# Attention and an MLP on one core: v loaded first, zeros for TensorE, new bounds for w_out, a new order

## The chip, the cores and the metric

The kernel runs on one NeuronCore of one Trainium2 chip. The metric is the device time of one execution in microseconds, as the median of a few runs. The engines work side by side and wait for each other by semaphores: TensorE (PE in the profile; its weight loads are PEld), VectorE (DVE), ScalarE (ACT), GpSimd (POOL) and SyncE (SP), which here issues all DMAs.

## The reference

```python
# q, k, v: 4 batches, 12 heads, 448 rows, 64 columns, float32
scores = scale * np.matmul(q, k.transpose(0, 1, 3, 2))
scores = np.where(mask, -1000000000.0, scores)        # causal
scores = scores - np.max(scores, axis=-1, keepdims=True)
attn = np.exp(scores)
attn = attn / (np.sum(attn, axis=-1, keepdims=True) + 1e-09)
attn_out = np.matmul(attn, v)
x = attn_out.transpose(0, 2, 1, 3).reshape(1792, 768)
h = x @ w_in                                          # w_in: 768 x 2048, float64 in memory
g = h - np.tanh(h)
return g @ w_out                                      # w_out: 2048 x 768, float64 in memory
```

## The kernel before

**Numbers.** Every large product is made of float16 matmuls. An operand is scaled by a power of two and split into a high and a low float16 part (`split`: one pass for the high part, `scaled`, and one for the low one), and three products replace one (high x high, high x low, low x high). The scale needs a bound of the operand's size first. For x, v, q and k it is a reduction or a pass (`bound`) and a small matmul that carries the maximum across partitions (`over_partitions`), followed by `bound_scale`. For w_in and w_out it is `magnitudes`: groups of matmuls of the operand with itself into the bank `b_scales`, whose maximum VectorE reads; `root_scale` makes the scale of it. The weights lie in memory as 64-bit floats. `decode` turns a loaded piece (the tile `slot` or `e`) into 32-bit floats: one shift pass (VectorE, ScalarE or GpSimd), then twice one ScalarE pass (into the banks that the trace calls `b_s`) and one VectorE pass.

**Stages.** (1) `first_rows` for batches 0 and 1, the chunk `c`: attention of the first 128 rows of each batch, in float32, in units of four heads (three units per batch, six per chunk). A unit is four score matmuls in float32, of which the trace shows two records each, eight in all (`b_s<-g`), four softmax parts on VectorE and ScalarE, `inverse` of the sums, the multiplication by it (`p0`), four transposes into a bank, the copy out of it (`p0t`), four value matmuls (eight records) into a bank, and the split of the result into x (`x0`). One bank, `b_x`, takes the transposes and the values in turn. (2) `w_in_chunk`, eight times: load, decode, magnitudes, scale, split of 256 columns of w_in. (3) `first_rows` for batches 2 and 3, the chunk `c2`. (4) `mlp_g_first`: x times w_in for both chunks, tanh, the split of g (`g0`, `g2`). (5) `w_out_half`, twice: sixteen pieces of w_out in all. (6) `mlp2` of both chunks: g times w_out. (7) For each batch, attention of the other 320 rows (`prep`, `weights_unit`, `weights_last`, `values`), then x times w_in (`mlp_g`) and g times w_out. The inverses of the sums (`inverse`, 75 of them, 12 in the first rows) stand between the softmax and the split of the weights.

**Order.** The instructions are not issued as written. The class `Work` collects them, and `schedule` plays them on a model of the engines (prices in `cost`, latencies in `LAT` and others) and takes, on each engine, the operation of the lowest rank among those that are ready by then. The ranks come from `RANK`. Where an operation can run on several engines (`either`), the letters of `CFG` say which one takes each occurrence: V is VectorE, A ScalarE, G GpSimd. What the model yields is fixed in the program as the order of each engine's queue; the chip works each queue off in order. All loads go through SyncE's queue in that fixed order. Every instruction is issued at one line, 288 of the file, so the trace's rows are told apart by tile, not by line.

## Time and profile before

| | us |
|---|---|
| median of 3 runs (581.05 to 581.48) | 581.06 |
| the profiled execution | 579.8 |
| its span, first to last instruction | 578.1 |

| engine | busy us | share of the span | instructions |
|---|---|---|---|
| PE | 557.8 | 96% | 5296 |
| PEld | 382.2 | 66% | 5296 |
| DVE | 426.5 | 74% | 1207 |
| POOL | 341.9 | 59% | 428 |
| ACT | 286.5 | 50% | 751 |

The shares are means over the whole span, over stages with different limits. A matmul's own duration includes its way through the pipeline, so groups of them are best read from the start of one group to the start of the next. In the rows, `b_m` are the banks of the MLP's products, `b_s` those of scores (and of the decode), `b_x` that of transposes and values, `small` the small columns for scales and sums.

### The profile page before, as it was taken

Reading aid. Unit: us, or ns where it says so; the run is one execution under the profiler, and the core shown is the slowest. Engines: PE = TensorE matmul, PEld = TensorE weight load, DVE = VectorE, ACT = ScalarE, POOL = GpSimd, SP = SyncE. Lnnn points to the kernel's source line nnn. Section 1 sums busy time; section 2 is a strip of 40 time slices with the busy share of each in tenths; the row PEclk is TensorE's granted clock in tenths of the full one; section 3 lists DMA queues with packets and bytes.
Section 4 is the critical chain, followed back from the end, with each engine's and each line's share of the span. In section 5 each row is a group of like instructions: output and inputs, shape, how many; then the busy total and the mean of one; then the engine's idle time right before and its main releaser. Section 6 shows DMA issues by size and latency. Waiting matters only on the chain.

```text
span 578.1 us, 13879 instructions
## 1 busy us (share of the span) xinstructions
PE 557.8 (96%) x5296; PEld 382.2 (66%) x5296; DVE 426.5 (74%) x1207; ACT 286.5 (50%) x751; POOL 341.9 (59%) x428
## 2 busy tenths in 40 slices
PE   6789999999999999999999999999999999999997
PEld 4567888866565666766666766566776566776664
DVE  5899999989999999699969996958599382332000
ACT  6899785744766845562555341606445150332000
POOL 3548965633563878975887888487956930542000
PEclk9999999999999999999999999999999999999999
DMA  8998379835486774365544435946123354000100
GB/s 305 343 298 310 112 213 258 239 110 178 102 161 136 183 163 78 93 174 124 119 118 92 92 66 109 211 100 125 42 69 62 69 80 101 2 1 1 28 28 27
DMA packets 109283, 74.04 MB, mean 128 GB/s; under 512 B 89760, under 2 KB 93344, under 8 KB 108704
## 3 DMA queue, kind: packets, MB, share of 16 engines
q1 hardware_dynamic: 109216, 73.15, 49.7%
q8 instruction: 41, 0.67, 0.5%
q14 instruction: 26, 0.21, 0.1%
HBM read 45.61 MB, written 5.51 MB: 88 GB/s over the span
## 4 chain that ended last, share of the span: by engine, by line
PE 68%; DVE 14%; DMA 7%; POOL 4%; issue 3%; ACT 2%; SPq 1%; DVEq 0%; POOLq 0%; ACTq 0%
PE b_m L288 57%; PE b_x L288 5%; PE b_s L288 5%; DVE pn L288 3%; DVE slot L288 2%; DVE small L288 2%; DVE prob L288 1%; PE b_scales L288 1%; DMA e<-in_v_dram 1%; DMA slot<-in_first_dram 1%; DMA g<-in_first_dram 1%; DVE g L288 1%; DVE first L288 1%; POOL first L288 1%; DMA pt<-pn 1%
## 5 line engine op out<-in xcount | busy, mean ns | idle before, releaser
L288 PE MATMUL b_m<-x,w_in 128*128 128x320 f16 (+1 forms) x1728 | 229.6, 290 | 1.6 <-DVE small L288 1.0
L288 PEld LDWEIGHTS <-w_in 128*128 128x128 f16 x1728 | 165.9, 98 | 56.3 <-issue 7.8
L288 PE MATMUL b_m<-slot,g 128*128 128x384 f16 x1152 | 191.7, 326 | 0.6 <-DVE t L288 0.5
L288 PEld LDWEIGHTS <-g 128*128 128x128 f16 x1152 | 111.1, 98 | 76.5 <-issue 5.1
L288 ACT ACTIVATE prob<-prob,small 128x256 f32<-128x256 f32 (+2 forms) x102 | 58.5, 574 | 62.2 <-DVE small L288 62.2
L288 ACT ACTIVATE t<-b_m,small 128x320 f32<-128x320 f32 (+1 forms) x70 | 37.6, 537 | 63.1 <-PE b_m L288 56.0
L288 DVE SCALAR_TENSOR_TENSOR t<-b_m,small,t 128x320 f32<-128x320 f32 (+1 forms) x70 | 39.4, 564 | 30.9 <-ACT t L288 30.7
L288 DVE CUSTOM_DVE_ANT_0 prob<-b_s,mask,small 128x384 f32<-128x384 f32 (+1 forms) x87 | 44.9, 549 | 8.6 <-PE b_s L288 7.5
L288 DVE TENSOR_SCALAR small<-small 128x1 f32<-128x1 f32 (+5 forms) x190 | 43.4, 242 | 6.1 <-ACT o L288 5.2
L288 ACT ACTIVATE o<-b_m,small 128x384 f32<-128x384 f32 x21 | 12.0, 572 | 61.3 <-PE b_m L288 61.3
L288 POOL TENSOR_SCALAR prob<-prob,small 128x384 f32<-128x384 f32 (+2 forms) x46 | 29.2, 634 | 18.9 <-ACT pn L288 6.6
L288 POOL TENSOR_SCALAR t<-t,small 128x320 f32<-128x320 f32 (+1 forms) x41 | 25.6, 625 | 23.9 <-ACT g L288 12.3
L288 POOL TENSOR_TENSOR g<-t,g 128x320 f16<-128x320 f32 (+1 forms) x40 | 34.1, 852 | 3.3
L288 PEld LDWEIGHTS <-v 128*64 128x64 f16 x1296 | 31.1, 111 | 7.1 <-issue 7.1
L288 DVE SCALAR_TENSOR_TENSOR pn<-prob,small,pn 128x256 f16<-128x256 f32 (+2 forms) x45 | 33.7, 767 | 1.5 <-ACT pn L288 0.8
L288 DVE SCALAR_TENSOR_TENSOR slot<-b_s,e 128x384 int32<-128x384 int32 x64 | 33.7, 548 | 0.9 <-POOL e L288 0.4
L288 PE MATMUL b_m<-slot,first 128*128 128x384 f16 x192 | 33.9, 326 | 0.0
L288 PE MATMUL b_s<-k,q 64*128 64x256 f16 (+2 forms) x342 | 30.6, 317 | 0.1
L288 POOL TENSOR_SCALAR g<-t,small 128x320 f16<-128x320 f32 (+1 forms) x21 | 14.5, 690 | 27.3 <-DVE t L288 25.9
L288 PEld LDWEIGHTS <-first 128*128 128x128 f16 (+2 forms) x282 | 21.7, 98 | 13.4 <-issue 2.2
L288 POOL TENSOR_TENSOR pn<-prob,pn 128x384 f16<-128x384 f32 (+2 forms) x30 | 28.0, 934 | 2.5
L288 POOL TENSOR_SCALAR e<-slot 128x768 int32<-128x768 uint16 x19 | 20.0, 1050 | 14.3 <-DMA slot<-in_moe_w_in_dram 6.6
(165 smaller groups left out, 878.8 us busy)
## 6 DMA issues: line engine op xcount, KB each, us to landing
slot<-in_moe_w_in_dram SPq DMA_DIRECT2D x16, 768.0 KB, 6.3
slot<-in_qk_dram SPq DMA_DIRECT2D x18, 384.0 KB, 3.4
slot<-in_moe_w_out_dram SPq DMA_DIRECT2D x8, 768.0 KB, 4.5
e<-in_moe_w_out_dram SPq DMA_DIRECT2D x8, 768.0 KB, 4.5
e<-in_v_dram SPq DMA_DIRECT2D x3, 1536.0 KB, 6.9
out_dram<-o SPq DMA_DIRECT2D x24, 192.0 KB, 1.9
first<-in_qk_dram SPq DMA_DIRECT2D x6, 384.0 KB, 3.7
g<-in_first_dram SPq DMA_DIRECT2D x6, 256.0 KB, 4.9
```

What stands on the lines that cost most here:

```text
L288: getattr(self.eng[o["eng"]], method)(*args, **kw)
```

## The change

- `first_rows` issues both loads of v before those of q and k, with a rank of their own (`c0_v`, `c0b_v`). For the chunk `c` the transposes and values use three banks in turn (`b_x` and the two `b_m`); for `c2` still one.
- A memset on GpSimd and 32 matmuls of zeros, 128x256 in bfloat16, into a `b_m` bank, with the rank 1002.08, which is behind all others.
- The bounds of w_out: instead of `magnitudes` (six matmuls per piece) and a reduction of 128 columns, one pass over the decoded piece (128x768) by `bound`: the sum of the absolute values on ScalarE for 14 pieces, their maximum on VectorE for 2. Its scale comes from `bound_scale`.
- The magnitudes of w_in are added up in one block of 128 columns instead of two, so that the reduction behind them reads 128 columns instead of 256.
- Small operations (`h`, 48 of them, and `inverse`) can go to GpSimd: 11 and 27 do.
- The model's prices and latencies, the ranks, how far the model looks ahead, and the letters are new, and so is the order of all queues.

The letters, counted as VectorE / ScalarE / GpSimd:

| operation | count | before | after |
|---|---|---|---|
| `p0` | 12 | 1 / 0 / 11 | 0 / 0 / 12 |
| `p0t` | 12 | 0 / 12 / 0 | 12 / 0 / 0 |
| `x0` | 12 | 1 / 11 / 0 | 3 / 9 / 0 |
| `g0`, `g0_lo` | 8, 8 | 2 / 0 / 6, 2 / 0 / 6 | 8 / 0 / 0, 0 / 0 / 8 |
| `g2`, `g2_lo` | 8, 8 | 0 / 5 / 3, 6 / 0 / 2 | 0 / 1 / 7, 3 / 0 / 5 |
| `shift_in` | 16 | 0 / 0 / 16 | 1 / 2 / 13 |
| `shift_out` | 16 | 2 / 6 / 8 | 0 / 5 / 11 |
| `w_out`, `w_out_lo` | 16, 16 | 1 / 10 / 5, 13 / 0 / 3 | 1 / 15 / 0, 14 / 0 / 2 |
| `b_out` (new) | 16 | | 2 / 14 / 0 |
| `inverse`, first 12 | 12 | 1 / 11 / 0 | 7 / 3 / 2 |
| `inverse`, all | 75 | 31 / 44 / 0 | 28 / 20 / 27 |
| `h`, first 40 | 40 | 40 / 0 / 0 | 31 / 0 / 9 |
| `p`, `p_lo` | 90, 90 | 33 / 22 / 35, 44 / 0 / 46 | 22 / 29 / 39, 53 / 0 / 37 |
| `g`, `g_lo` | 64, 64 | 20 / 25 / 19, 26 / 0 / 38 | 18 / 33 / 13, 31 / 0 / 33 |

Some ranks (a lower one goes first):

| | before | after |
|---|---|---|
| loads of v, first chunk (`c0_v`) | with q and k | -74.7 |
| loads of q and k, batch 0, batch 1 | -83.3, -71.9 | -60.9, -30.5 |
| first four loads of w_in | -61.7 | -39.7 |
| first rows (`c0`), w_in | -66.6, -75.7 | -146.5, -108.4 |
| w_out, its split | -19.9, 15.5 | -41.2, 42.0 |
| attention of batch 0 (`att0`) | -23.2 | -58.5 |

```diff
-    LAT = {"A": 34.0, "V": 32.0, "G": 98.0, "T": 52.0, "S": 26.0}
-    NEXT = {"A": 100.0, "V": 82.0, "G": 22.0}
-    TURN = 94.0, 24.0
+    LAT = {"A": 40.0, "V": 35.0, "G": 105.0, "T": 52.0, "S": 26.0}
+    NEXT = {"A": 94.0, "V": 80.0, "G": 12.0}
+    SECOND = 84.0
+    FIRST = 25.0
+    TURN = 94.0, 10.0
...
+    idle = first_block[:, :P].bitcast(BF16)
+    G.memset(idle, 0.0)
+    rank(RANK["warm"])
+    for _ in range(CFG["warm"]):
+        T.matmul(banks[6][:, :2 * P], idle[:, :P], idle, start=True, stop=True)
+    rank(0)
...
+    def on_small(tag, *args):
+
+        wk.either(tag, lambda: V.tensor_scalar(*args), lambda: G.tensor_scalar(*args))
...
     def root_scale(us, s, acc, i, unit):
 
         V.tensor_reduce(us, over_partitions(acc, i, unit), axis=AX.X, op=ALU.max)
-        V.tensor_scalar(us.bitcast(I32), us.bitcast(I32), 2.0 ** 28, 8.0 / 9.0, ALU.max, ALU.mult)
+        on_small("h", us.bitcast(I32), us.bitcast(I32), 2.0 ** 28, 8.0 / 9.0, ALU.max, ALU.mult)
...
-        pm = bank_1[:, :2 * P]
-        magnitudes(pm, y, [[(cc, b) for cc in range(NCC)] for b in range(2)])
+        pm = bank_1[:, :P]
+        magnitudes(pm, y, [[(cc, b) for cc in range(NCC) for b in range(2)]])
...
-                decode(y, t, scratch(i, 2), "_out")
-                pm = bank_1[:, 3 * P:]
-                magnitudes(pm, y, [[(k, b) for k in range(2) for b in range(3)]])
-                V.tensor_reduce(acc[:, 2 * m + a:2 * m + a + 1], pm, axis=AX.X, op=ALU.max)
+                junk = scratch(i, 2)
+                decode(y, t, junk, "_out")
+                bound(acc[:, 2 * m + a:2 * m + a + 1], y.rearrange("p a b -> p (a b)"), junk.bitcast(F32), "b_out")
         a1, s = r_acc(), r_s1()
         V.tensor_reduce(a1, acc, axis=AX.X, op=ALU.max)
-        root_scale(us_out[:, n:n + 1], s, a1, 0, ident16)
+        bound_scale(us_out[:, n:n + 1], s, a1, 0, mx_w)
...
-        V.tensor_scalar(c.ch[:, j], us_in[:, j], c.us_x, None, ALU.mult)
-        V.tensor_scalar(c.sg[:, j], c.ch[:, j], 2.0 ** 15, 2.0 ** -100, ALU.mult, ALU.max)
+        on_small("h", c.ch[:, j], us_in[:, j], c.us_x, 1.0, ALU.mult, ALU.mult)
+        on_small("h", c.sg[:, j], c.ch[:, j], 2.0 ** 15, 2.0 ** -100, ALU.mult, ALU.max)
...
-                  lambda: A.activation(total, total, AF.Copy, scale=factor, bias=1e-9 * factor))
+                  lambda: A.activation(total, total, AF.Copy, scale=factor, bias=1e-9 * factor),
+                  lambda: G.tensor_scalar(total, total, 1e-9, factor, ALU.add, ALU.mult))
...
-    def first_rows(c, bs, blocks, xs, name):
+    def first_rows(c, bs, blocks, xs, name, bank_x):
 
         qkf = [view(block, at, [NP, 2, P], F32) for block, at in blocks[:2]]
         vf = view(*blocks[2], [2, NP, 2 * D], F32)
+        rank(RANK[name + "_v"])
+        for i, b in enumerate(bs):
+            S.dma_start(vf[:, i].rearrange("p n d -> p (n d)"), first[b, :, NP * 2 * P:])
         for i, b in enumerate(bs):
             rank(RANK[name + "_load"] + i * RANK[name + "_next"])
             for g in range(H // 4):
                 pairs = slice(2 * g, 2 * g + 2)
                 S.dma_start(qkf[i][:, pairs].rearrange("p n x t -> p (n x t)"), first[b, :, g * 4 * P:(g + 1) * 4 * P])
-            S.dma_start(vf[:, i].rearrange("p n d -> p (n d)"), first[b, :, NP * 2 * P:])
...
-    first_rows(c, (0, 1), [(g_block, i * 8 * H * D) for i in range(3)], 0, "c0")
+    first_rows(c, (0, 1), [(g_block, i * 8 * H * D) for i in range(3)], 0, "c0", Ring([banks[4], banks[5], banks[6]]))
-    first_rows(c2, (2, 3), [(TS[5 + i], 0) for i in range(3)], 1, "c0b")
+    first_rows(c2, (2, 3), [(TS[5 + i], 0) for i in range(3)], 1, "c0b", bank_x)
...
-AHEAD = {"A": 85.6, "G": 32.5, "S": 149.2, "T": 1.2, "V": 93.4}
+AHEAD = {"A": 0, "G": 0, "S": 0, "T": 12.8, "V": 57.9, "hold": 0}
```

## Rows read from the trace of the kernel before

**Rows 1.** Windows: length, busy us (xcount) of PE, PEld, DVE, ACT, POOL; clock, DMA.
```profile
0.00:3.60 3.60, 0.00 (x0) 0.00 (x0) 1.28 (x5) 1.28 (x1) 1.55 (x8) 1.00 0.46 143
3.60:29.90 26.30, 20.43 (x123) 15.57 (x123) 19.23 (x86) 20.50 (x72) 11.95 (x11) 1.00 0.98 344
29.90:48.80 18.90, 15.32 (x165) 11.82 (x161) 18.43 (x73) 18.01 (x50) 11.51 (x9) 1.00 0.94 326
48.80:123.10 74.30, 72.63 (x725) 62.62 (x723) 72.17 (x195) 53.44 (x111) 48.49 (x45) 1.00 0.64 193
...
200.00:574.40 374.40, 373.22 (x3586) 246.98 (x3583) 244.20 (x648) 141.08 (x382) 227.18 (x306) 1.00 0.39 84
```

**Rows 2.** Timeline of TensorE, first 40 us: start, us, operation, shapes, count.
```profile
13.37 1.76 PE L288 MATMUL b_s<-g 64*128 64x128 f32 x8 [0.59 <-DVE small L288]
...
32.37 0.82 PE L288 MATMUL b_m<-x,w_in 128*128 128x256 f16 x6
...
39.96 0.66 PE L288 MATMUL b_x<-pt,g 128*64 128x128 f32 x8
```

**Rows 3.** The chain that ended last, to 135 us: start, us, what.
```profile
64.27 0.69 PE b_scales L288 x12
64.96 1.31 PE b_m L288 x12
...
74.37 0.34 PE b_scales L288 x6
...
75.30 0.65 PE b_s L288 x8
...
77.36 0.44 PE b_x L288 x4
...
78.80 0.59 PE b_x L288 x8
...
121.40 1.02 DVE slot L288 x2
```

**Rows 4.** Waits of VectorE, 0 to 29.9 us: total us, times, longest.
```profile
DVE pn L288 <- PE b_s L288: 4.6, 3, 2.7
```

**Rows 5.** Waits of TensorE, same stretch.
```profile
PE b_x L288 <- ACT pt L288: 3.1, 2, 2.2
```

**Rows 6.** Groups of VectorE (DVE), 0 to 123.1 us: xcount, busy us, mean ns.
```profile
L288 DVE SCALAR_TENSOR_TENSOR slot<-b_s,e 128x384 int32<-128x384 int32 x64 | 33.7, 548 | 0.9 <-POOL e L288 0.4 <-ACT b_s L288 0.4
...
L288 DVE CUSTOM_DVE_ANT_0 pn<-b_s,mask 128x128 f32<-128x128 f32 x48 | 11.7, 281 | 5.0 <-PE b_s L288 4.9
...
L288 DVE TENSOR_REDUCE small<-b_scales 128x1 f32<-128x128 f32 x27 | 7.6, 282 | 1.4 <-PE b_scales L288 1.3
...
L288 DVE TENSOR_SCALAR small<-small 128x1 f32<-128x1 f32 x36 | 5.3, 174 | 0.1
...
L288 DVE SCALAR_TENSOR_TENSOR t<-b_m,small,t 128x512 f32<-128x512 f32 x5 | 3.7, 743 | 0.0
...
L288 DVE TENSOR_REDUCE small<-g 128x1 f32<-128x1536 f32 x1 | 1.8, 1753 | 0.7 <-DMA g<-in_first_dram 0.7
...
L288 DVE TENSOR_SCALAR g<-t,small 128x512 f16<-128x512 f32 x1 | 0.5, 485 | 0.0
```

**Rows 7.** Groups of ScalarE's instructions, same stretch.
```profile
L288 ACT ACTIVATE pt<-b_x 128x512 f32<-128x512 f32 x12 | 7.0, 586 | 0.2 <-PE b_x L288 0.2
...
L288 ACT ACTIVATE slot<-slot,small 128x768 f16<-128x768 f32 x3 | 2.8, 929 | 0.0
```

**Rows 8.** Loads of the first rows: time from issue to landing.
```profile
DMA to landing us min/median/max: 2.8/6.2/7.8
```

**Rows 9.** Groups of GpSimd's instructions, 0 to 123.1 us.
```profile
L288 POOL TENSOR_SCALAR pt<-pt,small 128x512 f32<-128x512 f32 x1 | 2.2, 2202 | 0.0
L288 POOL TENSOR_SCALAR pn<-pn,small 128x512 f32<-128x512 f32 x3 | 2.1, 692 | 0.2
...
L288 POOL TENSOR_SCALAR_AFFINE_SELECT mask_last<-mask_last 64x64 f32<-64x64 f32 x2 | 0.5, 234 | 0.1
```

More of the change, by code (lines that the diff above doesn't have):

```diff
@@ L200, in schedule @@
         wrote = read = -1e9
-        moved, since, last, warm, mode = 0.0, 0.0, 0.0, False, (True, True)
+        moved, since, last, warm, mode = 2200.0, 0.0, 0.0, False, (True, True)
         half = None
@@ L213, in schedule @@
         while len(order) < n:
-            t, e = min((next_at(e), e) for e in engines if ready[e] or waiting[e] or half is not None and half[1] == e)
+            t, e = min((next_at(e) - self.FIRST * (e == "G"), e) for e in engines if ready[e] or waiting[e] or half is not None and half[1] == e)
+            t += self.FIRST * (e == "G")
             part = 0
@@ L263, in schedule @@
                     o["start"] = t
-                    free[e] = end + self.LAT[e]
+                    free[e] = end + self.SECOND
                     half = free[e], e, i
```

32 lines of the change are left out of this document (21 added, 11 removed).

## The prediction

> **What bounds the kernel now.** The profiled execution took 579.8 us around a span of 578.1 us; the sum below is made against the 579.8. The median of the three runs shown is 581.06 us, 1.26 us above it, and that difference is added at the end. A change of less than 0.2% (1.2 us) can hardly be told from none here.
>
> I read the busy time by stretches first [rows 1]. From 48.8 us on TensorE hardly stops: 72.63 of 74.3 us up to 123.1 us, and 373.22 of 374.4 us after 200 us. After 200 us it is thus idle for 1.2 us before its last matmul. So after the first fifty microseconds the kernel is as long as TensorE's list of matmuls, and it gets shorter only by work taken off that list or by an earlier start of the full stretch. The start is poor. Until 48.8 us TensorE is idle for 3.6 + 5.87 + 3.58 = 13.05 us [rows 1].
>
> Some of its busy time there is slow time too. Eight score products of the first rows take 1.76 us at 13.4 us and 0.65 us at 75.3 us [rows 2, 3]. The column of the granted clock says 1.00 in all stretches, so the level is read from the durations: 1.2 GHz until about 29.9 us, 2.4 GHz behind it. What ran before 29.9 us was 7 groups of eight score products, 4 of four transposes, 3 of eight value products, 2 of twelve magnitude products and 3 single matmuls. At the later prices 0.65, 0.44, 0.59, 0.69 us [rows 3], and with next to nothing for the single ones, these are 9.5 us, not 20.43. The slow clock thus costs 10.9 us, and TensorE has lost 24.0 us by 48.8 us.
>
> Not all of that can come back, because VectorE is the second bound: 18.43 of 18.9 us busy from 29.9 us, 72.17 of 74.3 us after it [rows 1]. The first matmul on w_out starts at 123.1 us, and the chain that leads there runs through VectorE's passes on w_out [rows 3], while TensorE has just used up its other work. Before 29.9 us VectorE has slack: it waits 4.6 us for score products and TensorE waits 3.1 us for transposed weights [rows 4, 5].
>
> **The change, part by part.**
>
> *w_out's bounds.* Sixteen groups of six magnitude matmuls go, at 0.34 us each [rows 3]: 16 x 0.34 = 5.4 us off TensorE. All lie before 123 us among matmuls that follow without a gap, so on TensorE they count in full. VectorE loses 16 reductions at 0.28 us, 4.5 us [rows 6]. In their place come 14 passes on ScalarE and 2 on VectorE over 128x768. ScalarE's 128x768 pass takes 0.93 us [rows 7], so 13 us plus the read of the sum; VectorE's 128x1536 reduction takes 1.75 us, so 0.9 us each. ScalarE was busy 53.44 of 74.3 us in that stretch, and it loses the evacuations below, so the passes have room on average. If that cover is gone, tanh is late, the two output banks stay full and TensorE stops.
>
> *Loads.* The two pieces of v, 0.79 MB, go ahead of q and k. At the 344 GB/s of the first stretch [rows 1] that moves the first score product from 3.6 to 5.9 us, since a load's shortest time to landing is 2.8 us [rows 8]. The bound of v (1.75 us, [rows 6]), now in the midst of the first unit, is worked off in this time. By the new ranks three pieces of w_in also pass the second batch's q and k: 0.79 + 0.79 + 2.36 + 0.26 = 4.2 MB must land first, so these arrive at about 0.8 + 2.0 + 12.2 = 15 us (2.0 us being the shortest landing less the piece's own transfer). The first batch's three units fill the time until then if each takes some 3 us. Nothing stalls by this, and little if it is 1 us late.
>
> *Zeros on TensorE.* 32 matmuls of 256 columns, ready after a memset. Twelve of that width take 1.31 us at the high level [rows 3], 0.11 each, so 0.22 at the low level. From about 1.3 us to the first data 21 fit; the other 11 cost from 0 (in gaps, as their rank puts them last) to 2.4 us (all ahead of the first product). I take 0.5 us. If they raise the clock, the 10.9 us become time in which TensorE is free, and each score product releases VectorE about a microsecond earlier.
>
> *Three banks.* Now one bank carries the transposes and then the values of each unit; the next unit waits for two evacuations. First x matmul on w_in at 32.4 us, last value product of the first chunk at 40.0 us [rows 2]. A unit of first rows at the high clock needs 0.65 + 0.44 + 0.59 = 1.7 us of TensorE and some 2.7 us of VectorE: four softmax passes at 0.28, two small operations at 0.17, an evacuation at some 0.65, x's low part and a quarter of its high part at 0.48 [rows 6]. With three banks the latter can set the pace: six units from 5.9 us on are 22 us, and the last one's way through TensorE and ScalarE ends some 3 us later, near 25 us, if no decode of w_in comes between.
>
> *VectorE's account up to w_out.* Counting the letters of the new assignment: 12 evacuations of 128x512 move from ScalarE, where they took 0.59 us, to VectorE. Its 128x512 rows are 0.48 us (from SBUF) and 0.74 us (from PSUM, two inputs) [rows 6]; I take 0.65, so +7.8 us (5.8 to 8.9). Six g splits at 0.48 us: +2.9. Five low splits less at 0.74: -3.7. Two reductions of w_out: +1.8. Six inversions at 0.17: +1.0, nine small operations to GpSimd: -1.6. Reductions of magnitudes: -4.5. The remaining shifts and splits about -1.0. Net +2.7 us. Against it stand VectorE's 9.9 us of idleness before 48.8 us (48.8 less 1.28 + 19.23 + 18.43). About 3 us of it must stay, until the first scores; of the 4.6 us wait for scores half goes with the clock, and another 1 us with the banks. That is 3.4 us back.
>
> So from TensorE's side the early part could give up to 10 us (24.0 less 5.9 at the start, less some 8 us in which units leave TensorE half idle). From VectorE's side it gives 3.4 - 2.7 = 0.7 us, unless w_out's second half is put behind the start of the w_out matmuls. I take 3.5 us with the 0.5 us of zeros in it: nearer VectorE's end, because the nearest row is the one at 98% busy.
>
> *Small operations on GpSimd, order.* After 200 us GpSimd is busy 227.18 of 374.4 us. The nearest prices there are 0.23 us (64x64) and 0.69 us (128x512) [rows 9]; VectorE's small one is 0.17 us [rows 6]. I take the lower end, the shape nearer to one to eight columns. 27 of 75 inversions go there, two of them early. They relieve two engines and lengthen a chain that TensorE hardly waits for (1.2 us in 374 us, [rows 1]); hidden behind the matmuls queued, they cost nothing. I put 1.0 us on the whole new order, between -1.2 us (all waits gone) and +10 us (rival 4).
>
> The Trainium skill (GPSIMD Engine Reference, section 3.1) speaks against this part: it says elementwise work should stay on VectorE, as GpSimd takes about twice as long for it. The rows agree in sign: 0.69 against 0.48 us for 128x512, and 2.20 us in one case [rows 6, 9]. By twice VectorE's 0.17 us an inversion would take an estimated 0.34 us; were it exposed, 25 of them would cost 25 x (0.34 - 0.17) = 4.3 us and the sum would be 577.5 us.
>
> **The sum.** 579.8 - 5.4 - 3.5 + 1.0 = 571.9 us for a profiled execution, and with 1.26 us a median of about 573.2 us, 1.4% faster.
>
> **The rivals.**
>
> 1. *TensorE's own bound comes through:* clock and banks give the whole 10 us, and attention on batch 0, which the new ranks put ahead of w_out, fills what VectorE leaves open. 579.8 - 5.4 - 10 = 564.4, as a median 565.7 us. For: the 24.0 us lost. Against: VectorE at 97 to 98%.
>
> 2. *VectorE takes it back:* the removed matmuls become a wait at the first w_out matmul. Only VectorE's 0.7 us remain: 580.4 us, about the same (577 to 582). For: VectorE set that start, and it is given 2.7 us more. Against: w_out's second half (16 decodes at 0.55 us, 8.8 us) need not be done first.
>
> 3. *The zeros do not raise the clock, or it falls before the data is there:* then the change does not do what it says. v ahead costs its 2.3 us, the banks give back 1.5 us. -5.4 + 2.3 - 1.5 + 1.0 = -3.6, so 577.5 us. For: TensorE was busy for 20.43 of 26.3 us before the clock rose, and still slow at 13.4 us [rows 1, 2]. Against: it did rise while TensorE worked on, and zeros are fed without the pauses that came before.
>
> 4. *Slower: the inversions on GpSimd starve attention.* Each of 25 stands on the way from softmax to split, behind whatever GpSimd has begun: up to 0.69 - 0.17 us of its own and up to 0.7 us of waiting for one operation ahead, 25 x 1.2 = 30 us if all is exposed. From 0.32 us each on (7.9 / 25) the gain is gone; at a third exposed it is 10 us, 583.3 us or more. For: GpSimd is 61% busy and its operation of one shape took 0.69 to 2.20 us. Against: units already pass through GpSimd there, and TensorE was idle for 1.2 us.
>
> **Chances.** The forecast (569 to 577 us) 0.50; rival 1 0.13; rival 2 0.17; rival 3 0.10; rival 4 0.10. The range of 566 to 580.5 us leaves out half of rival 1, a quarter of rival 2 and rival 4. Faster by over 0.2% (under 579.9): the forecast, rivals 1 and 3, and half of rival 2, 0.80. Within 0.2%: the rest of rival 2, 0.08. Slower: rival 4 and the tails, 0.12.
>
> **What would show it.** The first score product near 6 us; the eight score products at 0.7 us from the second unit on; the first x matmul on w_in before 28 us and the last unit's values by 30 us; no magnitude products of w_out; the first w_out matmul between 112 and 117 us; after it a stretch of 455 us as long as before within 2 us. Wrong it is if the first w_out matmul still starts near 122 us with TensorE waiting for VectorE ahead of it (rival 2), if early products stay at 1.6 us (rival 3), or if TensorE's idle time after 200 us grows from 1.2 us to ten (rival 4).

## The result and the profile after

The changed kernel takes 587.17 us (median of 4 runs, 586.36 to 588.36) against 581.27 us for the kernel before beside it: a ratio of 1.0104 [1.0078, 1.013], 1.0% slower. The profiled execution was the longest of its four, 588.36 us around a span of 586.6 us. The forecast was 573.2 us.

To see where the time went I cut both traces at one state: the end of the last group of the chunk `c2`'s products with w_in. All products with w_in for the first rows are then done, and 4228 matmuls follow in either kernel. These are the groups (start, duration), first of the kernel before, then of the changed one, from the timeline of TensorE:

```profile
131.00 1.47 PE L288 MATMUL b_m<-x,w_in 128*128 128x256 f16 x12
```
```profile
133.91 1.47 PE L302 MATMUL b_m<-x,w_in 128*128 128x256 f16 x12
```

The cut lies at 132.5 us before and 135.4 us after: 2.9 us are lost ahead of it. The rest of the span is 578.1 - 132.5 = 445.6 us before and 586.6 - 135.4 = 451.2 us after: 5.6 us are lost behind it. (The expectations below count the cut 0.2 us earlier in both kernels and all experiments, by the modelled end of its last matmul.) Two places, then, and both had been forecast otherwise.

These two losses add up to 8.5 us, as the two profiled executions differ by that much; the medians differ by 5.9 us. How far they can be trusted shows in the profiles of the experiments below. The rest was 445.6 to 446.1 us in the four profiles with the late part of before (before, 8, 12, 16), and 448.9 to 451.2 us in the seven with the changed one (after, 1, 2, 5, 11, 13, 17), so the late loss is 3 to 5.6 us. The cut is less steady: two profiles whose queues are the same up to it have it 1.0 us apart (135.4 us in the changed kernel, 134.4 in experiment 14) and 1.4 us apart (132.5 us before, 133.9 in experiment 15). The early loss is then some 0.5 to 3 us, and a cut that differs by less than 1.5 us says nothing.

The windows of the changed kernel over the stretches of [rows 1], with the same columns; the last is as long as the one there and ends as far before the end:

```profile
0.00:3.60 3.60, 2.45 (x12) 1.77 (x13) 1.28 (x5) 1.28 (x1) 1.86 (x9) 1.00 0.45 142
3.60:29.90 26.30, 20.52 (x167) 14.97 (x166) 21.02 (x89) 16.44 (x63) 9.39 (x11) 0.81 1.02 371
29.90:48.80 18.90, 16.11 (x166) 13.00 (x165) 18.89 (x73) 18.40 (x46) 11.29 (x11) 0.99 0.81 254
48.80:123.10 74.30, 65.63 (x589) 54.93 (x587) 69.63 (x182) 59.34 (x125) 55.37 (x58) 0.93 0.68 202
208.50:582.90 374.40, 370.83 (x3515) 243.81 (x3512) 246.32 (x646) 146.17 (x383) 194.25 (x271) 1.00 0.38 83
```

Before, TensorE hardly stopped from 48.8 us on (72.63 of 74.3 us). Now it does 65.63 us there: 8.7 us idle, where products of 5.4 us are gone. In the last stretch it is idle for 3.6 us instead of 1.2.

The start, from the timeline of TensorE (start, duration, operation, shapes, count; in brackets the wait before it and what ended it):

```profile
1.15 4.82 PE L302 MATMUL b_m<-first 128*128 128x256 bf16 x29 [1.15 <-POOL first L302]
7.12 0.72 PE L302 MATMUL b_s<-g 64*128 64x128 f32 x8 [1.15 <-DMA g<-in_first_dram]
7.76 0.50 PE L302 MATMUL b_m<-first 128*128 128x256 bf16 x3
...
10.70 1.64 PE L302 MATMUL b_s<-g 64*128 64x128 f32 x8 [0.76 <-DVE small L302]
...
22.00 0.66 PE L302 MATMUL b_m<-pt,g 128*64 128x128 f32 x8
...
31.52 0.66 PE L302 MATMUL b_m<-pt,g 128*64 128x128 f32 x8
32.12 0.39 PE L302 MATMUL b_m<-x,w_in 128*128 128x256 f16 x2
33.42 0.83 PE L302 MATMUL b_m<-x,w_in 128*128 128x256 f16 x6 [0.91 <-DVE w_in L302]
```

The zeros do raise the clock: the first score products take 0.72 us, the duration of the high level. But at 10.70 us the next ones take 1.64 us again, the granted clock is 0.50 from 11.0 to 21.3 us, and the value products reach 0.66 us only at 22 us. The last values of the first chunk come at 31.5 us instead of 40.0 [rows 2], so the three banks work. The first product with w_in, though, starts at 32.1 us as before (32.4, [rows 2]). What holds it now is the other operand: the next group waits 0.91 us for VectorE's half of the split of w_in. This is VectorE's timeline, the kernel before first: the first softmax part, and the first of VectorE's eight passes that finish a split of w_in.

```profile
4.99 0.29 DVE L288 CUSTOM_DVE_ANT_0 pn<-b_s,mask 128x128 f32<-128x128 f32 x1 [2.75 <-PE b_s L288]
...
23.80 1.82 DVE L288 SCALAR_TENSOR_TENSOR w_in<-slot,small,w_in 128x1536 f16<-128x1536 f32 x1 [0.24 <-ACT w_in L288]
...
33.15 1.80 DVE L288 SCALAR_TENSOR_TENSOR w_in<-slot,small,w_in 128x1536 f16<-128x1536 f32 x1
...
65.36 1.81 DVE L288 SCALAR_TENSOR_TENSOR w_in<-slot,small,w_in 128x1536 f16<-128x1536 f32 x1
```
```profile
7.98 0.29 DVE L302 CUSTOM_DVE_ANT_0 pn<-b_s,mask 128x128 f32<-128x128 f32 x1 [1.14 <-PE b_s L302]
...
31.55 1.81 DVE L302 SCALAR_TENSOR_TENSOR w_in<-slot,small,w_in 128x1536 f16<-128x1536 f32 x1
...
36.90 1.94 DVE L302 SCALAR_TENSOR_TENSOR w_in<-slot,small,w_in 128x1536 f16<-128x1536 f32 x1
...
69.25 1.81 DVE L302 SCALAR_TENSOR_TENSOR w_in<-slot,small,w_in 128x1536 f16<-128x1536 f32 x1
```

The softmax starts 3.0 us later, the first split of w_in 7.8 us, the second 3.8 and the seventh 3.9 us later. TensorE, which was busy for 24.25 us from 50 to 75 us before, is busy for 18.00 us there. Its waits from 50 to 75 us in the changed kernel (total, times, longest):

```profile
PE b_scales L302 <- DVE small L302: 2.4, 1, 2.4
PE b_m L302 <- DVE pt L302: 2.1, 1, 2.1
PE b_m L302 <- DVE t L302: 1.4, 1, 1.4
PE b_scales L302 <- DVE slot L302: 0.9, 1, 0.9
```

Together these are 6.8 of 25 us, and all of them end with an output of VectorE. The first matmul on w_out starts at 125.3 us, where 112 to 117 was forecast and 123.1 was before.

### The profile page after: what moved, and what is told of

Same layout as the page of the kernel before. It is cut to its first block, busy times and chain, and to the rows that moved or that the text cites. A ratio compares the mean times of both kernels' runs of the same rounds, so it can differ in the third digit from the quotient of the medians.

```text
span 586.6 us, 13729 instructions
## 1 busy us (share of the span) xinstructions
PE 558.1 (95%) x5232; PEld 378.4 (65%) x5232; DVE 439.2 (75%) x1221; ACT 295.7 (50%) x751; POOL 305.8 (52%) x402
## 5 line engine op out<-in xcount | busy, mean ns | idle before, releaser
L302 PEld LDWEIGHTS <-w_in 128*128 128x128 f16 x1728 | 167.6, 98 | 62.2 <-issue 10.5
L302 PEld LDWEIGHTS <-g 128*128 128x128 f16 x1152 | 110.8, 98 | 74.3 <-issue 3.8
L302 ACT ACTIVATE prob<-prob,small 128x384 f32<-128x384 f32 (+2 forms) x102 | 58.4, 573 | 48.7 <-DVE small L302 48.2
L302 POOL TENSOR_SCALAR g<-t,small 128x320 f16<-128x320 f32 x13 | 7.9, 608 | 66.1 <-DVE t L302 65.4
L302 DVE TENSOR_SCALAR small<-small 128x2 f32<-128x2 f32 (+5 forms) x176 | 37.1, 226 | 1.1 <-ACT pn L302 0.8
L302 PEld LDWEIGHTS <-first 128*128 128x128 f16 (+3 forms) x314 | 25.8, 100 | 16.4 <-issue 2.5
L302 DVE SCALAR_TENSOR_TENSOR pn<-prob,small,pn 128x384 f16<-128x384 f32 (+2 forms) x50 | 33.9, 696 | 2.9 <-ACT pn L302 1.9
L302 DVE TENSOR_SCALAR o<-b_m,small 128x384 f32<-128x384 f32 x8 | 4.9, 613 | 40.8 <-PE b_m L302 40.8
L302 POOL TENSOR_SCALAR t<-t,small 128x320 f32<-128x320 f32 (+1 forms) x38 | 25.6, 672 | 18.0 <-ACT g L302 14.6
L302 POOL TENSOR_TENSOR g<-t,g 128x320 f16<-128x320 f32 (+1 forms) x36 | 32.4, 899 | 3.0
L302 POOL TENSOR_SCALAR prob<-prob,small 128x384 f32<-128x384 f32 (+2 forms) x34 | 21.7, 639 | 22.3 <-ACT pn L302 7.7
L302 PE MATMUL b_s<-k,q 64*128 64x256 f16 (+2 forms) x342 | 30.5, 317 | 0.3 <-DVE small L302 0.3
L302 POOL TENSOR_SCALAR small<-small 128x2 f32<-128x2 f32 (+4 forms) x38 | 11.8, 309 | 34.7 <-DVE small L302 19.2
```

The lines of the kernel that those rows point to most:

```text
L302: getattr(self.eng[o["eng"]], method)(*args, **kw)
```

## The experiments

Each ran beside the kernel before on the same chip; ratios are to it. "Cut" is the state above (132.5 us before, 135.4 us after) and "rest" the span behind it (445.6 and 451.2 us), each read from the one profile of the run. Where a line says "order kept", the queues of all engines are those of the kernel that was edited; only the named operations differ. Three of the edits change the numbers that are computed, which is said there.

**1. No zeros.** The memset and the 32 matmuls are not issued; order kept.

```diff
+            if o["rank"] == RANK["warm"] or i == 0:
+                continue
```

> The changed kernel without its memset and its 32 matmuls of zeros; the order of everything else is kept. The changed kernel took 587.2 us. Theory Z (the zeros shorten the start by their warm clock, although the clock falls again at 10.7 us): without them the products up to 22 us are slower by up to 1 us per group of eight for the first two groups, and the time is 588.5 to 590 us. Rival (VectorE, not TensorE, sets the pace until 75 us, so the zeros buy nothing): 586.5 to 588 us, and the first matmul of x on w_in within 0.5 us of 32.1 us.

585.36 us, 1.0073 [1.0054, 1.0093]: 1.8 us less than with the zeros. The cut comes at 133.8 us, and the value products reach 0.66 us at 20.1 us, earlier than with them. The zeros bought nothing, and they can hold up the first data: they stand first in TensorE's queue, and in six profiles with them (3, 5, 7, 9, 11, 14) the first score products start right behind the last of the 29 zeros, at 5.9 to 7.2 us. Without them they start when the load is there, at 5.7 us here and at 6.2 us in experiment 13.

**2. The copies of transposed weights (`p0t`) back on ScalarE,** order kept.

```diff
+            if o.get("tag", ("",))[0] == "p0t":
+                o["eng"] = "A"
```

> The changed kernel with the 12 evacuations of transposed weights in the first rows back on ScalarE, at the same places of the order. Theory V (VectorE's load paces w_in, and w_in paces TensorE until 75 us): VectorE loses some 7.8 us of work before 95 us, the last magnitude products of w_in move from 67.5 us to 62 to 64 us, and the time falls by 3 to 6 us, to 581 to 584 us. Rival O (the order itself leaves TensorE without work, whoever makes the copies): 586 to 588 us.

585.13 us, 1.0075 [1.0059, 1.0091]; cut at 133.1, rest 450.3 us. This gives some 2 us back, about a quarter of the work taken off VectorE (the interval just overlaps that of the changed kernel). TensorE's hole from 50 to 75 us stays (17.89 us busy).

**3. The 38 small operations back from GpSimd:** the 27 inversions on ScalarE, the 11 operations `h` on VectorE; order kept.

```diff
+            if o.get("tag", ("",))[0] in ("inverse", "h") and o["eng"] == "G":
+                o["eng"] = "A" if o["tag"][0] == "inverse" else "V"
```

> The changed kernel with the 38 small operations back from GpSimd, at the same places of the order: inversions on ScalarE, scales on VectorE. Theory G (the inversions on GpSimd lengthen the way of each attention unit, and that is TensorE's idle time of 5.5 us behind 135 us): the time falls by 3 to 5 us, to 582 to 584 us, and the idle time behind 135 us falls below 3 us. Rival (the small operations cost nothing; VectorE's greater share behind 150 us makes the idle time): 586 to 588 us, idle time as before.

588.1 us, 1.0126 [1.0109, 1.0143]; rest 450.5 us. Nothing is won. The inversions on GpSimd are not the cause of the late loss.

**4. The kernel before with passes instead of products for w_out,** all 16 on ScalarE at the place of the old reductions, which go; order kept.

```diff
+                wk.ops[-1]["drop"] = True
                 V.tensor_reduce(acc[:, 2 * m + a:2 * m + a + 1], pm, axis=AX.X, op=ALU.max)
+                wk.ops[-1]["pass"] = ((junk16, y.rearrange("p a b -> p (a b)"), AF.Abs), dict(accum_out=acc[:, 2 * m + a:2 * m + a + 1]))
...
-        root_scale(us_out[:, n:n + 1], s, a1, 0, ident16)
+        bound_scale(us_out[:, n:n + 1], s, a1, 0, mx_w)
```

> The kernel before with one part of the change alone: the bounds of w_out by 16 passes on ScalarE (sum of absolute values, written to a buffer of bytes), each at the place where VectorE's reduction stood; no magnitude products of w_out; the order of everything else is that of before. The kernel before took 581.3 us. Theory T (TensorE's list is the bound, as the prediction has it): 16 x 0.34 = 5.4 us less, 575 to 577.5 us. Rival (VectorE's chain to the first w_out matmul is the bound, and gives the time back as a wait): 579.5 to 582 us, with TensorE waiting for VectorE or ScalarE before 123 us.

590.26 us, 1.0162 [1.0144, 1.018]. The cut comes at 138.7 us. From 75 to 125 us ScalarE is busy for 42.50 us (before: 33.34), VectorE only for 39.80 (before: 47.94): it waits for ScalarE, the longest (4.1 us in all) for ScalarE's half of the decode.

**5. The changed kernel with the products and their reductions back,** at the place of the passes; order kept.

```diff
+            if "back" in o:
+                o["back"]()
+                continue
...
+        for n, (a, b) in enumerate((k, b) for k in range(2) for b in range(3)):
+            nc.tensor.matmul(pm, u[:, a, b * P:(b + 1) * P], r[:, a, b * P:(b + 1) * P], start=(n == 0), stop=(n == 5))
+        nc.vector.tensor_reduce(o, pm, axis=AX.X, op=ALU.max)
```

> The changed kernel (587.2 us) with the bounds of w_out as before: each pass of ScalarE is replaced, at its place of the order, by six magnitude products on TensorE and a reduction on VectorE; the order of everything else is kept. Theory L (TensorE's list counts in full, as the prediction has it): 16 x 0.34 = 5.4 us more, 591 to 594 us. Rival P (the passes cost ScalarE about 1.0 us each, 14 us in a stretch where VectorE waits for ScalarE, and that takes the gain back): 583 to 587 us.

592.03 us, 1.0183 [1.0135, 1.023], 4.9 us more than the changed kernel. There the exchange of products and reductions for passes is worth about what the products alone were forecast to be (5.4 us). The run does not tell how much of it is TensorE's time and how much VectorE's, which has the 16 reductions back.

**6. The kernel before without the products and their reductions,** 2 of the 16 pieces bounded by passes on ScalarE, the bound of the others taken as 0; order kept.

```diff
+            if "pass" in o and not o["first"]:
+                continue
...
+                wk.ops[-1]["first"] = m == a == 0
```

> The kernel before (581.0 us) without the magnitude products of w_out and their reductions, and with a pass on ScalarE for the first piece of each half alone, 2 of 16; the bound of a half is that of its first piece, which leaves out 14 of 16 bounds. The order of everything else is kept. The version with all 16 passes took 590.3 us. Theory L (TensorE's list is the bound and the passes alone cost the time): 575 to 577.5 us. Rival C (VectorE and the decode's chain set the start of the w_out products, and removed products turn into waits): 579.5 to 582 us, with TensorE idle for 3 us or more between 75 and 130 us.

583.68 us (10 runs), 1.0034 [1.0007, 1.0062]: no gain at all. The cut is at 132.5 us, as before. The first window below is of the kernel before, the other two are of this one:

```profile
75.00:125.00 50.00, 49.05 (x484) 41.26 (x481) 47.94 (x125) 33.34 (x72) 26.83 (x28) 1.00 0.69 200
```
```profile
75.00:125.00 50.00, 44.58 (x401) 36.73 (x402) 45.16 (x114) 35.03 (x77) 28.52 (x29) 1.00 0.70 206
150.00:450.00 300.00, 295.16 (x3082) 192.83 (x3081) 256.13 (x723) 152.26 (x436) 219.78 (x290) 1.00 0.56 116
```

From 75 to 125 us TensorE is idle for 5.4 us, before for 0.95. The removed work has become waiting time, mostly of products in the `b_m` banks for VectorE (3.6 us). But VectorE, which lost 16 reductions, is idle for 4.8 us there, too (before: 2.1). Work came off both engines, and the stretch was no shorter: neither's load alone set its length. What did is not shown; in this trace GpSimd waits for loads of w_out for 13.8 us of the 50 (before: 10.2), and the queue that issues the loads waits 19.0 us for ScalarE's decode of earlier pieces (before: 18.7). The rest is 449.4 us, 3.8 us longer than before, though no queue behind the cut was changed.

**7. The changed order with the old engines for the attention of the later rows.**

```diff
+            t, n = o.get("tag", ("", 0))
+            if t in OLD and (t != "inverse" or n >= 12):
+                o["eng"] = OLD[t][n % len(OLD[t])]
```

> The changed kernel with the engines of the kernel before for the splits, evacuations and inversions of attention and of the MLP behind it (all tags from q, k, v, p to g, x and o, and the inversions behind the twelfth), at the same places of the new order. In the stretch from the last x product of the first rows (135.2 us) to the end, of 4230 matmuls in both kernels, VectorE has 318.1 us of work against 308.1 before, and that stretch is 5.6 us longer. Theory V2 (VectorE's greater share makes TensorE wait there): that stretch shrinks by 2 to 5 us. Rival O2 (it is the order of the queues, which does not fit the engines now): it stays within 1 us or grows.

636.71 us, 1.0951 [1.0907, 1.0994]. The engines of `CFG` and the order belong together; old letters at new places cost 50 us. This run tells nothing of either by itself.

**8. The kernel before with three banks for the first four units,** order kept.

```diff
+                u = 3 * i + g
+                to = Ring([banks[4], banks[5], banks[6]])
+                to.i = 2 * u
+                pq, py = (to(), to()) if name == "c0" and u < 4 else (None, None)
```

> The kernel before (581.0 us) with one part of the change alone: the first four units of the first rows use three banks in turn instead of one (the other two units would meet the x products in the same banks); the order is kept. Theory B (one bank holds the units back): the first x product moves from 32.4 us to 29 to 31 us and the time falls by 1 to 2.5 us. Rival (the order of the queues, not the bank, sets the pace of the units): the first x product within 0.5 us of 32.4 us, the time within 1 us of 581.0.

582.4 us (10 runs), 1.0014 [0.999, 1.0038]. The banks alone give nothing, with the order of units as it was.

**9 and 10. The two plans crossed.** The 1953 operations made after the first rows keep the order and the engines of the other kernel, written out as a list; the operations made earlier follow their own plan.

```diff
+        late = [(k + i, e) for i, e in zip(LATE, LATE_ENG)]
...
+                for d in self.ops[i]["deps"]:
+                    while d not in done:
+                        put(*late[n])
+                        n += 1
+                put(i, self.ops[i]["eng"])
```

> The changed kernel, with the 1953 operations made after the first rows (from the output scale of the two first chunks on: attention of the other chunks, splits, output products) in the order and on the engines that they had before the change; the 9 us of the early part and all operations made earlier keep the changed order. Where a dependency needs a late operation earlier, it goes earlier. Theory K (the late order itself costs the 5.6 us that the changed kernel loses behind the common state, 451.4 against 445.8 us): the rest comes back to about 446 us and the kernel takes about 581.5 us. Theory P (the late part is only as bad as the state in which the early part leaves it, or the old late order does not fit the new early part): 587 us or more.

> The reverse: the kernel before, with those 1953 late operations in the changed order and on the changed engines (27 small ones that have no form for GpSimd there stay on their old engine). Theory K: the common state is reached as before, about 132.3 us, and the rest takes about 451 us, so about 586 us. Theory P: the rest stays at 446 us, 581 us in all.

9 takes 589.77 us, 1.0159 [1.0112, 1.0206]; 10 takes 589.96 us, 1.0149 [1.0126, 1.0172]. These are the windows from 150 to 450 us, in turn of the kernel before, the changed one, 9, and 10:

```profile
150.00:450.00 300.00, 298.14 (x3105) 195.01 (x3104) 260.16 (x729) 153.46 (x438) 222.69 (x294) 1.00 0.54 116
```
```profile
150.00:450.00 300.00, 294.46 (x3167) 190.69 (x3166) 275.19 (x782) 161.52 (x452) 208.57 (x289) 1.00 0.58 123
```
```profile
150.00:450.00 300.00, 298.57 (x3103) 194.70 (x3102) 258.36 (x731) 153.26 (x435) 218.17 (x284) 1.00 0.54 116
```
```profile
150.00:450.00 300.00, 293.08 (x3157) 189.56 (x3156) 275.19 (x790) 162.17 (x465) 200.60 (x263) 1.00 0.60 123
```

TensorE's idle time is 1.9, 5.5, 1.4 and 6.9 us: in these four it goes with the late plan, whatever came first. In 10 the rest takes 454.6 us. So theory K holds for this stretch. The late plan is not the only way to such idle time, though: experiments 4 and 6, with the late plan of before and with less work on VectorE there (258.40 and 256.13 us against 260.16), are idle for 4.3 and 4.8 us. Theory K fails for the sum: 9 loses at the junction of the two plans what it wins behind it. Its chain that ended last shows how:

```profile
125.17 7.61 DMA e<-in_v_dram
132.78 0.02 issue
132.80 3.35 DVE small L306
...
139.08 0.57 ACT o L306
139.65 0.04 issue
139.69 1.44 PE b_m L306 x4
```

The load of v for the later attention goes into one of the raw buffers of w_out (`e`). The load of the last piece of w_out into it is issued at 118.6 us in the changed kernel, at 116.8 us in 9 and at 111.8 us before. The old late plan puts the bound of that v (3.35 us of VectorE) ahead of work that TensorE waits for, and TensorE stands still for 5.9 us.

**11. The changed kernel with 2 of the 16 passes;** the bound of the other pieces is taken as 0; order kept.

```diff
+            if o.get("tag", ("",))[0] == "b_out" and o["tag"][1] % 8:
+                continue
```

> The changed kernel with 2 of the 16 passes that bound w_out; the bound of the other 14 pieces is left out (their maximum is taken as 0). No order changes. This takes 14 passes of about 0.95 us, some 13 us, off ScalarE and VectorE between 75 and 120 us. Theory S (the passes on ScalarE hold up the early part): the common state comes 2 to 3 us earlier, at about 132.5 us, and the kernel takes about 584.5 us. Theory R (w_out's two raw buffers and their loads set the pace of that stage, whatever the bounds cost): 587 us, the loads still about 3.5 us apart.

586.0 us (7 runs, 582.25 to 586.92), 1.0065 [1.0039, 1.0091]. By the median the 14 passes cost 1.2 us, which can hardly be told from nothing: the interval overlaps that of the changed kernel. The profile is of the fastest run, so its cut (129.8 us) says little.

**12. The kernel before with a third raw buffer for six pieces of w_out,** order kept.

```diff
+                if 2 <= i < 8:
+                    t3 = view((ES[1], ES[2], TS[0])[i % 3], 0, [2, HALF], I64)
```

> The kernel before with a third raw buffer for pieces 2 to 7 of w_out, order kept. Theory R (the two raw buffers set the pace of w_out's stage): the loads of these pieces come under 3 us apart instead of 3.4, the first matmul on w_out starts 2 to 4 us before 123.1 us, and the kernel takes about 578.5 us. Rival (VectorE and ScalarE set that pace): 581 us, the first matmul on w_out as before.

580.06 us (10 runs), 0.999 [0.9971, 1.001]. The six loads are issued 2.0 to 5.5 us earlier than before, but the last load of w_out still at 111.5 us (before: 111.8). Theory R falls for these pieces: a buffer more does not make the stage faster. VectorE is busy for 24.75 of 25 us from 75 us on, but that its load sets the pace is not shown by this, and experiment 6 speaks against it.

**13. Less early work on VectorE in the changed kernel, and no zeros;** order kept.

```diff
+            if tag[0] == "p0t":
+                o["eng"] = "A"
+            if tag[0] == "g0":
+                o["eng"] = "GGGGGGVV"[tag[1]]
+            if tag[0] == "shift_in":
+                o["eng"] = "G"
```

> The changed kernel without the zeros, and with three kinds of early operations taken off VectorE and put on the engines that had them before the change: the 12 copies of transposed weights (ScalarE), 6 of the 8 first halves of the split of g (GpSimd), and the one shift of w_in that had gone to VectorE (GpSimd). No order changes. That is 7.5 us or so off VectorE before 75 us, where it is busy 65.1 of 75 us and TensorE 18.0 of 25. Theory V (in the early part the change put more on VectorE than it took off, so w_in is split later and TensorE stands still from 50 to 75 us): the common state comes at about 130.5 us instead of 135.2, the kernel takes about 581.5 us. Rival (the order itself holds w_in back): no better than the copies alone, about 133 us and 585 us.

586.96 us, 1.0109 [1.0087, 1.013]; cut at 135.0 us. VectorE is busy for 58.9 us up to 75 us instead of 65.1, and TensorE gets nothing of it (16.55 of 25 us from 50 to 75). Theory V falls. VectorE now waits itself, 2.3 us for GpSimd's shifts and 1.6 us for magnitudes. The first split of w_in starts at 30.9 us, the seventh at 69.5, almost as in the changed kernel (31.55 and 69.25): it is their place in the order that is late.

**14. The changed kernel with 21 of VectorE's low parts in the late attention left out;** their readers use what the buffer held. Order kept.

```diff
+            if o["eng"] == "V" and o.get("tag", ("",))[0] in ("p_lo", "p_first_lo", "k_lo", "q_lo", "v_lo"):
+                self.lows = getattr(self, "lows", -1) + 1
+                if self.lows % 3 == 2 and 12 < self.lows < 75:
+                    continue
```

> The changed kernel with 21 of VectorE's second halves of splits in the attention of the later chunks left out (every third one, about 0.8 us each, some 16 us between 180 and 400 us); their readers use what the buffer held. No order changes. Theory D (the late part is longer because 15 us of its work went from GpSimd to VectorE, which is then busy 92% from 150 to 450 us): TensorE's idle time from 150 to 450 us falls from 5.5 to about 2 us and the rest behind the common state from 451.4 to about 448 us, 584 us in all. Theory O (the order puts short chains of single operations ahead of TensorE, whatever VectorE's load): 587 us, idle as before.

584.25 us, 1.0065 [1.0048, 1.0083]; rest 448.3 us. The window:

```profile
150.00:450.00 300.00, 295.79 (x3189) 192.72 (x3187) 267.24 (x764) 162.59 (x454) 202.57 (x288) 1.00 0.58 124
```

TensorE is idle for 4.2 us instead of 5.5. Of the 5.6 us lost in the rest 2.9 come back; against the other profiles with the same late plan and queues (450.2 to 450.7 us in 1, 2, 11 and 13) it is some 2 us.

**15. The kernel before with 20 such low parts issued twice.**

```diff
+                if self.lows % 3 == 2 and self.lows < 60:
+                    for method, args, kw in o["alts"]["V"][0]:
+                        getattr(self.eng["V"], method)(*args, **kw)
```

> The other way round: the kernel before with 20 such second halves issued twice on VectorE, some 15 us more for it between 150 and 440 us, results the same. No order changes. Theory D: TensorE's idle time from 150 to 450 us rises from 1.9 to about 5.5 us, the rest from 445.8 to about 449.5 us, the kernel takes about 584.7 us. Theory O: the two pauses of TensorE stay as they are, 581 us.

590.53 us, 1.017 [1.0141, 1.02]; rest 454.7 us, idle 7.5 us from 150 to 450 us. This is more than theory D said (590.5, not 584.7): 15 us more on VectorE cost 9 us there. In the order of before VectorE's passes in the late part have little slack. Both experiments change the number of passes, which stand on the way from the scores to the values, so load and length of that way change together.

**16. The kernel before with the two loads of v first,** nothing else.

```diff
-        for i in self.schedule():
+        order = self.schedule()
+        v = [i for i in order if self.ops[i].get("v_load") == "c0"]
+        for i in v + [i for i in order if i not in v]:
```

> The kernel before with the two loads of v of the first two batch elements issued ahead of their q and k, and nothing else changed. Theory F (the first softmax starts when q and k have landed, and what VectorE and ScalarE do for the first rows and for w_in stands behind it in their order, so a later start is paid for nearly in full): VectorE takes the first scores at about 7.5 us instead of 4.99, the first splits of w_in and the common state come 2 to 3 us later, the kernel takes about 583.5 us. Rival (the slack of the first 25 us, where VectorE waits 5 us for scores, swallows it): 581 us.

582.65 us (9 runs), 1.0059 [1.0034, 1.0084]; cut at 134.6 us, rest 445.6 us. VectorE's timeline in this kernel:

```profile
7.16 0.29 DVE L290 CUSTOM_DVE_ANT_0 pn<-b_s,mask 128x128 f32<-128x128 f32 x1 [4.92 <-PE b_s L290]
...
25.90 1.82 DVE L290 SCALAR_TENSOR_TENSOR w_in<-slot,small,w_in 128x1536 f16<-128x1536 f32 x1 [0.24 <-ACT w_in L290]
...
67.17 1.82 DVE L290 SCALAR_TENSOR_TENSOR w_in<-slot,small,w_in 128x1536 f16<-128x1536 f32 x1
```

The softmax starts 2.17 us later, the first split of w_in 2.10, the seventh 1.81, the cut 2.15 us later, and the medians differ by 2.35 us. Next to nothing of the delay is swallowed on the way, though VectorE waits for scores for 4.6 us in that stretch before [rows 4]; it now waits for them for 6.8 us. These waits are part of the chain, not slack beside it.

**17 and 18. The changed kernel without zeros, v loaded behind q and k and its bound 14 operations later;** 18 with the old late plan as well.

```diff
+            if i in chain:
+                spot.setdefault(n + 14, []).append(i)
...
+            if i == qk[len(qk) // 2 - 1]:
+                out.append(v[0])
+            if i == qk[-1]:
+                out.append(v[1])
```

> The changed kernel without the zeros, with v of each of the first two batch elements loaded behind its q and k again, and with v's bound (one reduction, its transposes and small operations) 14 operations of VectorE later, so that it stands behind the first unit's softmax. Everything else keeps its order. Theory F: VectorE's first softmax starts at about 5 us instead of 7.98, the splits of w_in and the common state come 3 to 4 us earlier (131.5 to 132 us, no longer behind the kernel before), and the late loss of 5.6 us stays: about 583.5 us. Rival (the new order of units and w_in holds the early part back by itself): the common state at 133.8 us as without the zeros alone, 585.4 us.

> The same early part with the late operations in the order and on the engines that they had before the change. With the changed early part this stood still for 5.9 us at 133 us, because the loads of v for the later attention wait for w_out's raw buffers, which come free 7 us later than before; an early part 3.5 us ahead leaves about 3 us of that. Theory F with theory K: about 580.5 us, the kernel before reached again. Rival (the junction does not close): 584 us or more.

592.89 us, 1.0187 [1.0162, 1.0213], and 598.1 us, 1.0272 [1.0237, 1.0307]. Both miss, by my edit: three loads of w_in stayed ahead of the second half of v, and VectorE, with everything behind the bound in its queue, stood for 6.0 us waiting for it. The softmax did start at 4.94 us. These runs show what a late v costs in this order (the cut at 141.3 us), and leave open whether the changed kernel's early part can be had back by its loads alone.

No version was faster than the kernel before by more than the runs can tell.

## Why the prediction was wrong

**w_out's products, 5.4 us.** The size was about right in the changed kernel (4.9 us for the whole exchange, experiment 5), the step was not, so that the size fits is luck. "On TensorE they count in full", because the matmuls there follow without a gap, is refuted by experiment 6: the same products, and the reductions behind them, taken out of the kernel before gave 0.0 us at the cut. TensorE without a gap from 75 to 125 us did not mean that it set the time. The removed matmuls became waits, as rival 2 had it. But rival 2's reason, that VectorE set the start of the products with w_out, is only half shown. The last passes ahead of that start are VectorE's in both traces, from about 117 us on, but VectorE's load does not set it: VectorE was busy for 47.94 of these 50 us before and for 45.16 without the reductions, and the first product with w_out came at 123.2 us as before. What sets it stays open. The cover that I named for the passes (ScalarE has room on average) did not hold either: at a place not planned for them the cut came 6.2 us later with all 16 passes than with two (138.7 us in experiment 4, 132.5 in 6). At their own place 14 of them cost 1.2 us by the medians (experiment 11).

**The early part, -3.5 us.** This term failed most. With the products back the changed kernel is at the cut at 140.1 us, 4.7 us later (experiment 5), and before it was there at 132.5: by these profiles the rest of the early change costs some 7.6 us, give or take 1.5, instead of giving 3.5.
- *v first:* I let the first scores be 2.3 us later and had the bound of v "worked off in this time". The first is right: 5.8 us against 3.6 with v first alone (experiment 16); in the changed kernel it is 7.1 us. That this is no loss is wrong: in experiment 16 all of it arrives at the cut, 2.15 us.
- *Zeros:* the clock rose, as forecast, and fell again at 10.7 us. That is rival 3, with the clock falling after the data is there. The 32 matmuls, put at 0.5 us, cost 1.8 us (experiment 1; the two intervals just overlap). The forecast set 1.76 us for a group of scores against 0.65; the first is a group's own duration, the second the step to the next group. In the first measure it is 1.76 against 0.71 us.
- *Three banks:* the units did become shorter, to 31.5 us for the last values (30 forecast). But the step from there to "first x matmul before 28 us" forgot the other operand. The order now puts units ahead of w_in on VectorE, the first split of w_in ends at 33.4 us instead of 25.6, and TensorE waits for weights.
- *VectorE's account:* its sum was a fair one (its gains add up to 3.3 us, not 3.4), but a sum was the wrong measure. Taking 6 us off VectorE changed nothing (experiment 13). I put this down to the fixed order of the queues and to the chain units, decode, scale, split, which runs through all engines; no run takes that chain apart.

The prices found for single edits (2.15, 1.8 and 2.0 us for v, zeros and copies) don't add up in a common run: experiment 13, with the zeros and the copies undone together, kept neither gain.

**Order and small operations, +1.0 us (up to +10).** It was 5.6 us in the first pair of profiles (3 to 5.6 over all), and for another reason than rival 4's. The inversions on GpSimd cost nothing that shows (experiment 3). The Trainium skill (GPSIMD Engine Reference, section 3.1) would keep such work on VectorE; taking it off GpSimd again, the inversions to ScalarE and the rest to VectorE, gave no gain, 588.1 against 587.2 us. In 9 and 10 the idle time behind 150 us goes with the late plan. I had counted letters of late operations (`p_lo` and `g_lo` 14 more on VectorE, `p` and `g` 13 fewer) and not summed busy time. From 150 to 450 us VectorE goes from 260.16 to 275.19 us of work, 92% busy, GpSimd from 222.69 to 208.57. Taking 21 of VectorE's passes out gave 2 to 2.9 us back (14), putting 20 in cost the kernel before 9 us (15). That passes on VectorE cost time there is shown, and the changed plan has more of them. It is not the whole cause. Single short chains (`b_scales` waiting for VectorE's small operations, 1.9 us) are argued from the waits. And experiments 4 and 6 lost 4 us in the rest with the old late plan and no more work on VectorE, mostly in the same kind of wait (3.7 and 4.3 us): how the early part hands over plays a role, too, and how much of the changed kernel's late loss is of that kind stays open.

"After it a stretch of 455 us as long as before within 2 us" was the sign that answers this term. It counts from the first product with w_out: 455.0 us before, 461.3 us in the changed kernel, 6.4 us longer.

## What to carry to other kernels

An engine without gaps need not be the bound: here two engines were busy for 98% and 96% of a stretch, work came off both, and it was no shorter. Before counting removed work in full, look at what the other engines do in that same stretch, ask what the relieved engine would do in the time won, and take the work out alone to see. With queues worked off in order, moving an early load or a unit moves all that stands behind it on every engine, so follow the other operand of the product that is to start earlier, not only the one that the change speeds up. And when a plan is replaced as a whole, sum the busy time per engine over the long steady stretch first: here 15 us went onto an engine that was 87% busy, and the span behind the cut became 3 to 5.6 us longer, as much as the start had promised to win. Last, a split of a loss between two places that rests on one pair of profiles needs a second pair: here the late share moved by more than 1 us.

## What the runs showed of the hardware

- TensorE's clock came up within 4.8 us of zeros (score products at 0.72 us, the duration at 2.4 GHz) and was down to 1.2 GHz at 10.7 us (1.64 us), after a stretch of short groups with pauses of 0.2 to 0.8 us between them. In the changed kernel it fell twice more: the granted clock is 0.5 from 48.6 to 52.0 us, after pauses of 0.78 and 0.64 us, and from 62.2 to 69.1 us, with pauses of 0.95, 2.40 and 2.13 us around the fall (twelve magnitude products at 67.5 us took 1.48 us; at the high level, at 64.1 us in the kernel before, 0.85). The Trainium skill (TensorE: Matmul & The Clock Gate, section "HAM oscillation — how this bites in real kernels") describes such a fall and rise for a kernel whose bursts of matmuls wait for loads. The fall and rise are here, too; around the two later falls the waits are for VectorE, the longest 2.40 us.
- The page of the changed kernel shows it in its slices of the span, as the granted clock in tenths. In the kernel before this row is 9 in every slice, though its products before 29.9 us take the low level's time (1.76 us at 13.4 us, [rows 2]): a 9 at the start of a trace is no proof of the high level, the durations are.

```profile
PE   7899589999999999999989999999999999999997
...
PEclk8798799999999999999999999999999999999999
```

- The kernel before took 578.6 to 584.5 us in the 68 runs beside the experiments, against 581.05 to 581.48 in its first three, so a difference under 2 us between medians of four runs says little.
